# Induced attention and a leaky feed-forward layer: the x blocks of the first pass are loaded from GpSimd's queue instead of SyncE's

## The chip, the cores and the metric

The kernel runs on one core of a Trainium2 chip. The metric is the device time of one execution in microseconds (us). TensorE (PE) multiplies, VectorE (DVE) and ScalarE (ACT) work on tiles, GpSimd (POOL) does a little elementwise work, and SyncE (SP) issues transfers. Each engine takes its own instructions in the order in which they are written; between engines there are semaphores.

## The reference

For each of 4 batches, 32 inducing rows attend over 12,480 tokens and give h; then all tokens attend over the 32 rows of h. The result goes through a feed-forward layer with a leaky ReLU.

```
def mab(q, kv):                       # q: rows x 128, kv: rows x 128
    s = (q @ kv.T) / sqrt(128)
    a = softmax(s)                    # over the rows of kv, 1e-9 added to the sum
    return a @ kv
h = mab(inducing, x)                  # first pass: 32 x 128 per batch
y = mab(x, h)                         # second pass: 12480 x 128 per batch
g = y @ w_in                          # 128 -> 2048
out = maximum(0.01 * g, g) @ w_out    # 2048 -> 128
```

All inputs and outputs are float32: x is 4 x 12480 x 128, `inducing` 32 x 128, `w_in` 128 x 2048, `w_out` 2048 x 128.

## The kernel before

The tokens of a batch are cut into six groups of 2048 and a rest of 192 (RG). A tile of the feed-forward part is 512 tokens, and the hidden width of 2048 is cut into 16 slices. One unit of work u is one slice of one tile: a product into PSUM (`ph`, L705), its positive part on ScalarE (`ghi`, L718), the remainder on VectorE (`glo`, L726), and three products into the output accumulator (`po`, L744). Products run LOOK = 3 units ahead: `ph` has three PSUM buffers, so the product of a unit can't start before VectorE has read the one three units earlier.

The attention of the next batches is woven into these units. For batch 0 an order written out by hand (ORDER) sets every step up to unit 48, and its x comes through `start` (L833). For batches 1 to 3 there are lanes of generators, each stepped once per unit in the main loop (L1217 to L1242): `scores` (the function `first_scores`), `values`, `seconds`, `stacking`, `fetches`, `stores`. A step that yields HEAVY adds to a debt that holds the lanes back for some units. Since the program is written in that order, the place of an instruction in its engine's queue is fixed.

The first pass needs x turned, with its 128 channels on the partitions. `load_blocks` reads x in blocks: for one half of a group (two of its four j) and four bands of 32 channels it issues eight transfers, each of 32 partitions x 16 x 32 elements (64 KB, in runs of 32 elements, 128 B); for RG twelve of 32 x 2 x 32 elements (8 KB). VectorE then turns 32 x 32 squares (`xTr` L389, `xT` L395). The tiles `xc` have three buffers. `first_scores` asks for three halves at once when it begins (RG and the first two: 12 + 16 = 28 transfers) and for one more half after each half that has been turned. That makes 324 transfers in three batches.

The steps of other lanes that the prediction speaks of: in the second pass, GpSimd subtracts the row maximum (`y<-y,mx`, L597), ScalarE takes the exponential (L603), VectorE sums and inverts (`sm`, L607 to L610), GpSimd multiplies (`y<-y,sm`, L612), and VectorE turns the result (`aT`, L621). GpSimd also makes the low parts of the attention weights (`alo`, L644), which SyncE spreads over partitions into `A`. In the first pass GpSimd moves maxima and sums between partition bands in copies of a few elements: `four<-rm` (L303), read by VectorE in L306 or L309; `nm<-nm` (L314), read by ScalarE; `four<-zn` (L497), read by VectorE in L498; `rz<-rz` (L502), read by ScalarE in L509.

SyncE's queue has all transfers but one: rows of x for the value products (L220), the blocks (L248), the spread of `A` (L656) and of `hws` (L560), and the stores of the output (L791). GpSimd issues none.

Of the kernel before, what the change touches and what calls it, by code (L numbers as in the profile page):

```python
# [20 lines left out]
def induced_attention_then_leaky_ffn(  # L21
# [20 lines left out]
    nc = tc.nc  # L42
# [153 lines left out]
    def rows_of(b, g):  # L196
        base, J, K = GROUPS[g]
        return x[b][base : base + 32 * J * K, :]
# [42 lines left out]
    def load_blocks(b, g, j0, nj):  # L241

        _, J, K = GROUPS[g]
        t = sb.tile([P, 32, 32], F32, tag="xc", name="xc", bufs=3)
        src = rows_of(b, g).rearrange("(j r k) c -> r j k c", j=J, k=K)
        for cb in range(NB):
            for j in range(nj):
                nc.sync.dma_start(  # L248
                    t[32 * cb : 32 * cb + 32, j * K : (j + 1) * K, :],
                    src[:, j0 + j, :, 32 * cb : 32 * cb + 32],  # L250
                )
        return t
# [107 lines left out]
    def first_scores(b):  # L360
# [5 lines left out]
        def more():  # L366
            if halves:
                h = halves.pop(0)
                blocks[h] = load_blocks(b, *h)
# [909 lines left out]
```

## Time and profile before

| | |
|---|---|
| median of 3 runs | 1496.11 us (1496.09 to 1496.35) |
| profiled execution | 1496.72 us, span of its instructions 1494.6 us |
| TensorE busy | 1480.1 us, 99% of the span |
| VectorE, ScalarE, GpSimd busy | 85%, 67%, 8% |
| chain that ended last | TensorE 95%, DMA 2%, VectorE 1% |
| block loads (L248) | 324 issues on SyncE, from 100.7 to 874.4 us |

Busy time is the share of the span in which an engine works on an instruction. Waiting, and issuing a transfer, does not count as busy; so GpSimd's 8% is tile work alone.

### The profile page before, as it was taken

The page shows a single profiled execution, that of the slowest core. Times are in us where ns is not written, and L with a number is a line of the kernel's source. Part 1 is how long each engine was busy: PE and PEld are TensorE (multiplying, and loading weights), DVE is VectorE, ACT ScalarE, POOL GpSimd, SP SyncE. Part 2 cuts the span into 40 slices and gives each one's busy share as a digit, 9 for nine tenths or more (in the row PEclk, how much of TensorE's full clock was granted, in tenths as well). Part 3 has the DMA queues.
Part 4 walks back from the last instruction along what each step waited for, and adds up shares of the span by engine and source line. Part 5 has one row for each costly group of instructions (what it writes and reads, how often), then busy time and mean ns, then how long its engine had stood idle before and what let it go on. Part 6 is the DMA issues. An engine that isn't in the chain of part 4 may idle for free.

```text
span 1494.6 us, 22249 instructions
## 1 busy us (share of the span) xinstructions
PE 1480.1 (99%) x7861; PEld 1262.8 (84%) x7861; DVE 1265.5 (85%) x2137; ACT 999.6 (67%) x1748; POOL 112.4 (8%) x182
## 2 busy tenths in 40 slices
PE   8999999999999999999999999999999999999998
PEld 6788888888889888888888888888888898888887
DVE  6888898879898898789899898798888888888886
ACT  5766666666676666676676666676766766666665
POOL 1300100000100100000010100010100000000000
PEclk9999999999999999999999999999999999999999
DMA  8127446335444432243533531231212212212211
GB/s 285 44 56 137 82 78 158 61 59 95 82 103 82 111 82 50 43 96 69 110 69 68 135 67 19 43 73 20 50 34 38 43 25 49 43 24 48 41 26 22
DMA packets 402079, 105.23 MB, mean 70 GB/s; under 512 B 372624, under 2 KB 375088, under 8 KB 401968
## 3 DMA queue, kind: packets, MB, share of 16 engines
q1 hardware_dynamic: 401920, 103.80, 33.7%
q8 instruction: 62, 1.02, 0.3%
q14 instruction: 49, 0.40, 0.1%
q10 hardware_dynamic: 48, 0.02, 0.0%
HBM read 48.94 MB, written 25.56 MB: 50 GB/s over the span
## 4 chain that ended last, share of the span: by engine, by line
PE 95%; DMA 2%; DVE 1%; SPq 1%; ACT 0%; issue 0%; POOL 0%; DVEq 0%; ACTq 0%
PE po L744 67%; PE ph L705 23%; PE s_ps L262 3%; PE po L763 1%; PE h_ps L438 1%; DMA xr<-in_x_dram 1%; DMA raw<-in_moe_w_out_dram 0%; DMA raw<-in_moe_w_in_dram 0%; SPq L248 0%; SPq L833 0%; PE w_ps L1069 0%; DVE glo L726 0%; ACT ghi L718 0%; DMA xc<-in_x_dram 0%; PE hw_ps L545 0%
## 5 line engine op out<-in xcount | busy, mean ns | idle before, releaser
L718 ACT ACTIVATE ghi<-ph 128x512 fp32r<-128x512 f32 (+1 forms) x1568 | 929.5, 595 | 463.7 <-PE ph L705 458.5
L726 DVE SCALAR_TENSOR_TENSOR glo<-ph,ghi 128x512 fp32r<-128x512 f32 (+1 forms) x1568 | 1041.9, 679 | 185.4 <-ACT ghi L718 163.0
L705 PE MATMUL ph<-A,hws 128*128 128x512 f32 (+1 forms) x1600 | 596.6, 377 | 1.6 <-DVE glo L726 1.3
L744 PE MATMUL po<-ghi,w_hi 128*128 128x512 f32 (+1 forms) x1568 | 593.7, 379 | 0.0
L744 PE MATMUL po<-glo,w_hi 128*128 128x512 f32 (+1 forms) x1568 | 593.1, 378 | 0.0
L744 PE MATMUL po<-ghi,w_lo 128*128 128x512 f32 (+1 forms) x1568 | 593.0, 378 | 0.0
L705 PEld LDWEIGHTS ph<-A,hws 128*128 128x128 f32 x1600 | 301.9, 189 | 59.3 <-DVE glo L726 5.6
L744 PEld LDWEIGHTS po<-glo,w_hi 128*128 128x128 f32 x1568 | 296.4, 189 | 41.9 <-DVE glo L726 0.7
L744 PEld LDWEIGHTS po<-ghi,w_lo 128*128 128x128 f32 x1568 | 296.3, 189 | 41.1
L744 PEld LDWEIGHTS po<-ghi,w_hi 128*128 128x128 f32 x1568 | 296.4, 189 | 39.9 <-ACT ghi L718 0.2
L773 DVE STREAM_TRANSPOSE osb<-po 128x512 f32<-128x512 f32 (+1 forms) x98 | 68.8, 702 | 1.5 <-PE po L763 1.5
L644 POOL TENSOR_TENSOR alo<-aT,ahi 128x512 fp32r<-128x512 f32 x22 | 28.1, 1279 | 486.1 <-ACT ahi L639 451.4
L395 DVE STREAM_TRANSPOSE xT<-xc 128x512 f32<-128x512 f32 x72 | 50.5, 701 | 1.6 <-DMA xc<-in_x_dram 1.6
L597 POOL TENSOR_TENSOR y<-y,mx 128x512 f32<-128x512 f32 x23 | 24.2, 1051 | 278.5 <-DVE mx L595 218.7
L612 POOL TENSOR_TENSOR y<-y,sm 128x512 f32<-128x512 f32 x23 | 24.1, 1049 | 189.1 <-DVE sm L610 159.9
L763 PE MATMUL po<-A,m2s 128*128 128x512 f32 (+1 forms) x100 | 37.1, 374 | 0.0
L355 DVE STREAM_TRANSPOSE y<-s_ps 128x512 f32<-128x512 f32 x22 | 15.7, 715 | 10.8 <-PE s_ps L262 9.2
L262 PE MATMUL s_ps<-xT,indT 128*32 128x512 f32 x192 | 24.2, 595 | 0.5 <-ACT xT L871 0.5
L262 PE MATMUL s_ps<-xT,hT 128*32 128x512 f32 x192 | 24.0, 597 | 0.4 <-ACT hT L1013 0.4
L763 PEld LDWEIGHTS po<-A,m2s 128*128 128x128 f32 x100 | 18.9, 189 | 2.6
L280 DVE TENSOR_SCALAR_CACHE_REDUCE e<-s_ps 128x512 f32<-128x512 f32 x18 | 12.4, 690 | 8.3 <-PE s_ps L262 7.5
L438 PE MATMUL h_ps<-xr,ay 128*32 128x128 f32 x576 | 17.6, 274 | 0.0
(152 smaller groups left out, 376.6 us busy)
## 6 DMA issues: line engine op xcount, KB each, us to landing
xr<-in_x_dram SPq DMA_DIRECT2D x96, 256.0 KB, 5.1
out_dram<-osb SPq DMA_DIRECT2D x384, 64.0 KB, 2.2
xc<-in_x_dram SPq DMA_DIRECT2D x288, 64.0 KB, 2.7
A<-ahi SPq DMA_DIRECT2D x188, 64.0 KB, 2.0
A<-alo SPq DMA_DIRECT2D x188, 64.0 KB, 2.0
hws<-hilo SPq DMA_DIRECT2D x64, 64.0 KB, 2.0
raw<-in_moe_w_in_dram SPq DMA_DIRECT2D x4, 512.0 KB, 7.8
raw<-in_moe_w_out_dram SPq DMA_DIRECT2D x4, 512.0 KB, 8.3
```

The lines of the kernel that those rows point to most:

```text
L262: nc.tensor.matmul(dst, lhsT, rhs, start=True, stop=True)
L395: nc.vector.transpose(t[:, j, :], blk.rearrange("p n c -> p (n c)"))
L438: nc.tensor.matmul(hp[32 * k : 32 * k + 32, :C], ay[:rows, 4 * q + k, :], xb[:rows, k, :], start=(i == 0 and q == 0), stop=(last[k] == i a ...
L597: engines[0].tensor_tensor(out=yv, in0=yv, in1=mx[:rows, :K].unsqueeze(2).broadcast_to([rows, K, M]), op=ALU.subtract,)
L612: engines[1].tensor_tensor(out=yv, in0=yv, in1=smv.unsqueeze(2).broadcast_to([rows, K, M]), op=ALU.mult)
L644: (engine or nc.gpsimd).tensor_tensor(out=alo[sl], in0=aT.pop((b, g))[: 32 * J, :], in1=ahi[sl].bitcast(F32), op=ALU.subtract,)
L705: nc.tensor.matmul(ph[:, o : o + w], hw[b][1][:, f * P : (f + 1) * P], woven(A4[t][:, o : o + w], t), start=True, stop=True,)
L718: nc.scalar.activation(halves(ghi[:, :n], t)[1], live[u][2], AF.Relu)
L726: nc.vector.scalar_tensor_tensor(out=halves(glo[:, :n], t)[1], in0=ph, scalar=0.0, in1=halves(ghi[:, :n], t)[1].bitcast(F32), op0=ALU.max, ...
L744: nc.tensor.matmul(accs[t][:, :n], w[:, f, :], woven(r[:, :n], t), start=(f == 0 and w is w_hi and r is live[u][0]), stop=False,)
L763: nc.tensor.matmul(accs[t][:, o : o + w], hw[b][2], woven(a4[:, o : o + w], t), start=False, stop=(o + w == n),)
L773: nc.vector.transpose(osb[:, :n], po[:, :n])
```

## The change

The block loads are issued by GpSimd instead of SyncE. Nothing else is written differently: the same 324 transfers stand at the same places of the program, but now in GpSimd's queue.

```
         for cb in range(NB):
             for j in range(nj):
-                nc.sync.dma_start(
+                nc.gpsimd.dma_start(
                     t[32 * cb : 32 * cb + 32, j * K : (j + 1) * K, :],
                     src[:, j0 + j, :, 32 * cb : 32 * cb + 32],
                 )
```

The instructions of TensorE, VectorE and ScalarE keep their order. On GpSimd, where batch 1's loads begin (`xc` is the block tile, `y` and `yr` the scores of the second pass for a full group and for RG, `mx` and `sm` their maxima and inverse sums):

```order
 L612 TENSOR_TENSOR y<-y,sm 128x512
 L597 TENSOR_TENSOR y<-y,mx 128x512
+L248 DMA xc<-in_x_dram 32x2x32 x12
+L248 DMA xc<-in_x_dram 32x16x32 x16
 L612 TENSOR_TENSOR y<-y,sm 128x512
 L597 TENSOR_TENSOR yr<-yr,mx 96x64
+L248 DMA xc<-in_x_dram 32x16x32 x16
 L612 TENSOR_TENSOR yr<-yr,sm 96x64
+L248 DMA xc<-in_x_dram 32x16x32 x8
 L644 TENSOR_TENSOR alo<-aT,ahi 128x512
+L248 DMA xc<-in_x_dram 32x16x32 x16
 L597 TENSOR_TENSOR y<-y,mx 128x512
```

The multiplication L612 of a tile now stands behind the 28 loads with which batch 1 begins. On GpSimd, where batch 2's loads begin (`nm` and `zn` are batch 1's negated maximum and its sum, `rz` the inverse of the sum):

```order
 L303 TENSOR_SCALAR four<-rm 32x2 x4
 L314 COPY nm<-nm 32x1 x3
+L248 DMA xc<-in_x_dram 32x2x32 x12
+L248 DMA xc<-in_x_dram 32x16x32 x16
 L497 COPY four<-zn 32x1 x4
 L502 COPY rz<-rz 32x1 x3
```

The 28 loads stand between the copies of the maximum and the copies of the sum; it is the same where batch 3's begin. On SyncE, at the place of batch 1's first loads (`out_dram` is the output, `osb` its tile, `xr` the rows for the value products):

```order
 L791 DMA out_dram<-osb 256x2x32 x8
-L248 DMA xc<-in_x_dram 32x2x32 x12
-L248 DMA xc<-in_x_dram 32x16x32 x16
 L220 DMA xr<-in_x_dram 96x256
 L220 DMA xr<-in_x_dram 128x512 x6
 L791 DMA out_dram<-osb 256x2x32 x4
 L220 DMA xr<-in_x_dram 128x512 x2
```

The rows and stores behind the loads move up by 28 places.

## Rows read from the trace of the kernel before

**Rows 1.** The page, part 1: busy us (share of the span) and instructions of each engine.
```profile
PE 1480.1 (99%) x7861; PEld 1262.8 (84%) x7861; DVE 1265.5 (85%) x2137; ACT 999.6 (67%) x1748; POOL 112.4 (8%) x182
```

**Rows 2.** Busy time by stretch: start:end, length, then engines, clock, DMA share, GB/s.
```profile
core 0: us, PE busy (x) PEld busy (x) DVE busy (x) ACT busy (x) POOL busy (x), PEclk, DMA share, GB/s
...
95.00:320.00 225.00, 223.94 (x1243) 190.16 (x1243) 197.41 (x347) 149.28 (x264) 18.18 (x41) 1.00 0.49 95
320.00:620.00 300.00, 300.00 (x1642) 256.36 (x1642) 261.61 (x451) 200.49 (x356) 25.46 (x49) 1.00 0.42 83
620.00:960.00 340.00, 339.93 (x1811) 288.86 (x1813) 294.20 (x497) 227.85 (x398) 26.17 (x48) 1.00 0.37 75
```

**Rows 3.** Waits, all engines: who waited for whom, us in total, times, longest.
```profile
DVE xT L395 <- DMA xc<-in_x_dram: 1.6, 1, 1.6
...
ACT ahi L639 <- DMA A<-ahi: 1.4, 1, 1.4
```

**Rows 4.** Line L248: ns min/median/max of an issue on SyncE, first and last start.
```profile
L248 SPq DMA_DIRECT2D xc<-in_x_dram x324: 571/625/3000, 100.7 to 874.4; - x162
```

**Rows 5.** DMA issues: KB each, median us from issue to landing.
```profile
xc<-in_x_dram SPq DMA_DIRECT2D x288, 64.0 KB, 2.7
```

**Rows 6.** Timeline of GpSimd: start us, us, line, [idle before <-releaser].
```profile
99.34 1.05 POOL L597 TENSOR_TENSOR y<-y,mx 128x512 f32<-128x512 f32 x1 [35.58 <-PE po L744]
105.31 1.05 POOL L612 TENSOR_TENSOR y<-y,sm 128x512 f32<-128x512 f32 x1 [4.92 <-DVE sm L610]
...
131.07 0.29 POOL L612 TENSOR_TENSOR yr<-yr,sm 96x64 f32<-96x64 f32 x1 [15.68 <-DVE sm L610]
140.49 1.28 POOL L644 TENSOR_TENSOR alo<-aT,ahi 128x512 fp32r<-128x512 f32 x1 [9.13 <-ACT ahi L639]
160.28 1.05 POOL L597 TENSOR_TENSOR y<-y,mx 128x512 f32<-128x512 f32 x1 [18.51 <-DVE mx L595]
161.41 1.06 POOL L303 TENSOR_SCALAR four<-rm 32x3 f32<-32x3 f32 x4
...
200.48 1.28 POOL L644 TENSOR_TENSOR alo<-aT,ahi 128x512 fp32r<-128x512 f32 x1 [13.59 <-ACT ahi L639]
...
240.85 0.61 POOL L314 COPY nm<-nm 32x1 f32<-32x1 f32 x3 [4.48 <-DVE least L309]
...
297.44 0.61 POOL L314 COPY nm<-nm 32x1 f32<-32x1 f32 x3 [6.34 <-DVE least L309]
304.78 0.82 POOL L497 COPY four<-zn 32x1 f32<-32x1 f32 x4 [6.72 <-DVE zn L335]
...
592.11 0.61 POOL L314 COPY nm<-nm 32x1 f32<-32x1 f32 x3 [4.39 <-DVE least L309]
```

**Rows 7.** Timeline of all engines around the first place.
```profile
107.77 0.38 PE L705 MATMUL ph<-A,hws 128*128 128x512 f32 x1
...
108.56 0.70 DVE L621 STREAM_TRANSPOSE aT<-y 128x512 f32<-128x512 f32 x1
...
109.19 2.05 DVE L726 SCALAR_TENSOR_TENSOR glo<-ph,ghi 128x512 fp32r<-128x512 f32 x3
...
110.58 0.38 PE L705 MATMUL ph<-A,hws 128*128 128x512 f32 x1
```

**Rows 8.** Timeline of VectorE: the other instructions that read GpSimd's results, and L389.
```profile
117.41 0.37 DVE L389 STREAM_TRANSPOSE xTr<-xc 128x192 f32<-128x192 f32 x1
...
166.43 0.14 DVE L306 TENSOR_REDUCE nm<-four 32x1 f32<-32x12 f32 x1
...
316.93 0.13 DVE L498 TENSOR_REDUCE rz<-four 32x1 f32<-32x4 f32 x1
...
617.00 0.13 DVE L498 TENSOR_REDUCE rz<-four 32x1 f32<-32x4 f32 x1
```

**Rows 9.** Timeline of SyncE: the first block loads, and a spread of A.
```profile
100.73 19.27 SPq L248 DMA_DIRECT2D xc<-in_x_dram  x28
...
149.55 0.58 SPq L656 DMA_DIRECT2D A<-ahi  x1
```

More of the change, by code (lines that the diff above doesn't have):

```diff
@@ L247, in load_blocks @@
             for j in range(nj):
-                nc.sync.dma_start(
+                nc.gpsimd.dma_start(
                     t[32 * cb : 32 * cb + 32, j * K : (j + 1) * K, :],
```

## The prediction

> **What bounds the kernel now.** I read the page's busy times first, then the busy time by stretch, then the waits, and then the timelines of GpSimd and VectorE, because the change concerns a queue and a queue is read by who stands behind whom. TensorE is busy for 1480.1 of 1494.6 us and GpSimd for 112.4 [rows 1]. In the stretch in which the block loads run, from 95 to 960 us, TensorE has 1.06, 0.00 and 0.07 us that are not busy [rows 2]. So that stretch can hardly get shorter than it is; it can only get longer, if something makes TensorE wait. The loads keep nobody waiting: one transpose of VectorE waited once for a block, 1.6 us [rows 3].
>
> What makes TensorE wait is VectorE or ScalarE standing still, since both work in order. How long it can do without VectorE is read at 108.56 us [rows 7]: VectorE turns a tile there (0.70 us) and reaches its next `glo` at 109.19. That one frees the `ph` buffer filled at 107.77, which TensorE fills again at 110.58. The `glo` is done at about 109.19 + 0.68 = 109.87 (a third of the 2.05 for three). So 0.7 us of a halt are free and the rest stops TensorE. Time lost so isn't won back, as TensorE has no slack to catch up with.
>
> **The change, part by part.** *Removed:* 324 issues from SyncE, at a median of 625 ns [rows 4], about 200 us of its queue. Rows of x, stores and the spread of `A` behind them go out earlier. Who waits for these: ScalarE, 1.4 us in all, for a spread [rows 3]. TensorE's idle time in the stretch is 1.13 us [rows 2], so this is worth between 0 and 1.1 us; I take 0.
>
> *Added:* 324 issues on GpSimd. Its 8% says nothing of their cost; what counts is how long each holds the queue, p, and who stands behind. No row shows p. From below, the smallest GpSimd instructions follow each other at 1.06 / 4 = 0.27 us (L303) [rows 6], and SyncE takes 0.63 for this very load [rows 4]. From above: a load of 64 KB is 512 runs of 128 B, each to be described once to read and once to write; if GpSimd does that as two of its dearest passes over 512 elements, L644 at 1.28 [rows 6], p is 2.56. I take 1.05, the row of GpSimd's commonest pass over 512 elements (L597, L612), which lies nearest to the middle of 0.63 and 1.28, and the same for small loads, as a low bound and a high bound at SyncE differ little (571 and 625 ns).
>
> The Trainium skill ("DMA: Bandwidth & Descriptors", section Specifications) says that a transfer from GpSimd, whose descriptors are written by software, has its first byte after about 1 us, against about 0.6 from SyncE. The second agrees with the 0.63 us of rows 4; no run here shows the first. By it p would be 1.0 as an estimate, and the sum below 33.3 us instead of 37.4.
>
> Each load also waits for the load eight before it to land, as GpSimd's transfers share eight semaphores. Landing takes 2.7 us from SyncE [rows 5]; eight loads at 1.05 take 8.4, which covers it. If landing takes over 8.4 us, p rises to an eighth of it.
>
> *First place, batch 1 begins.* L597 ends at 99.34 + 1.05 = 100.39 [rows 6]. Then come 28 loads, then L612 (1.05), whose result VectorE needs at 108.56 for L621 [rows 7]. Before, L612 started at 105.31 and was in time. Now it ends at 101.44 + 28p, and with 0.7 us free, TensorE loses 28p - 7.8. At p = 1.05 that is 21.6 us.
>
> *Second place, batch 2 begins.* The copies of `nm` end at 297.44 + 0.61 = 298.05 [rows 6]. 28 loads, then L497 (0.82), which VectorE's L498 needs at 316.93 [rows 8]. Before, L497 stood there at 304.78, 11 us early. The loss is 298.05 + 28p + 0.82 - 316.93 - 0.7 = 28p - 18.8, that is 10.6 us.
>
> *Third place, batch 3 begins.* The same with 592.11 + 0.61 = 592.72 and 617.00 [rows 6, 8]: 28p - 24.2, that is 5.2 us. The stalls before shift all engines alike, so the differences hold.
>
> *Fourth place, batch 1's first maximum.* After the first stall everything is later by 28p - 7.8. The next loads wait for a block buffer that L389 frees, at 117.41 + 0.37 + 28p - 7.8 = 110.0 + 28p [rows 8]. Behind that GpSimd has 16 loads, L612 (0.29), 8 loads, L644 (1.28), 16 loads, L597 (1.05) and four copies L303 (1.06) [rows 6]: it ends at 113.7 + 68p. VectorE reads them in L306 at 166.43 + 28p - 7.8, with 0.7 free: 159.3 + 28p. The loss is 40p - 45.6, at p = 1.05 less than nothing, so 0; the cover is thin (3.6 us) and gone at p = 1.14. The spread of `A` behind L644 is in time: L644 ends at 111.5 + 52p = 166.1, SyncE comes to it at 149.55 + 21.6 = 171.2 [rows 9].
>
> *The other groups* have 8 to 24 loads between instructions of GpSimd that lie some 15 to 40 us apart; at 1.05 us a load I take 0. The tightest that I worked out, before batch 1's second maximum: L644 ends at 200.48 + 1.28 = 201.76, then come 24 loads, L597 (1.05) and four copies L303 (about 1.06 again), which VectorE's L309 reads just before 240.85 [rows 6]. With 0.7 free that binds from p = (240.85 + 0.7 - 203.9) / 24 = 1.57.
>
> Sum: 21.6 + 10.6 + 5.2 + 0 = 37.4 us on the profiled execution's own 1496.72, so 1534.1. That execution lies 0.6 above the median of the runs, which gives 1533.5.
>
> **The rivals.**
>
> *No change (the other side).* If an issue on GpSimd is as cheap as its smallest instruction, the first place loses 28 x 0.27 - 7.8 < 0 and so do the others: 1496, not slower. It decides at p = 7.8 / 28 = 0.28 us. For it: GpSimd is busy for 112 us of 1494.6 [rows 1], and a queue that only hands work on could be this quick. Against it: SyncE, with nothing else to do, takes 0.63 for the same load [rows 4]. A gain of over 0.2% (3.0 us, about what a measurement of this kernel can tell from no change) has no place to come from, as the idle time in the stretch is 1.1 us [rows 2].
>
> The Trainium skill (the same page, section Issuing engines are not separate DMA queues) says that spreading transfers over issuing engines saves only issue time, which is usually small. The 200 us taken off SyncE are that time, and rows 3 show nobody waiting for it. By that rule alone the result would be this rival.
>
> *GpSimd issues as fast as SyncE.* With p = 0.63 only the first place binds: 28 x 0.63 - 7.8 = 9.8 us, 1506. For it: the engine only tells the transfer engines what to do, and SyncE's time hardly depends on the size (571 to 625 ns). Against it: GpSimd's other instructions are slower than their counterparts, 1.05 us for a pass over 512 elements against VectorE's 0.70 [rows 6, 7].
>
> *The price grows with the runs.* 512 runs to read and 512 to write make p well above 1.28. Then the fourth place and the groups with 24 loads bind as well. At 1.28 the sum is 28.0 + 17.0 + 11.6 + 5.6 = 62 us; at 1.7 it is 39.8 + 28.8 + 23.4 + 22.4 + 24 x (1.7 - 1.57) = 117 us, 1614; at 2.56 it is 63.9 + 52.9 + 47.5 + 56.8 + 23.8 = 245 us, 1741. For it: these are the shortest runs in the kernel, and the count of 512 is far above a row load's. Against it: at SyncE the count of runs shows nothing.
>
> The Trainium skill ("SBUF — State Buffer", section SBUF: two separate sides) says that GpSimd can't write descriptors while VectorE runs an instruction in a two-port mode, which would lengthen p by up to one such instruction. The rows at 108 us show VectorE's passes over 512 elements at 0.68 to 0.70 us, none of them in half the time, so I give the rule no weight of its own.
>
> **How the numbers follow.** Between p = 0.8 and 1.35 (first place binding strongly, others partly) lies my forecast, with 0.55. GpSimd about as fast as SyncE, 0.4 to 0.8: 0.15. The price growing with the runs, above 1.35: 0.21. No change, below 0.38 (loss under 3 us): 0.06. A gain: 0.03, for something that I don't see. The likeliest case's own range is 0.8 to 1.35: the first place loses 14.6 to 30.0 us, the second 3.6 to 19.0, the third 0 to 13.6, the fourth 0 to 8.4, so 18 to 71 us, 1514 to 1567. The range that holds 8 in 10 goes from p = 0.57, SyncE's lowest row (28 x 0.57 - 7.8 = 8.2 us, 1504), to p = 1.7 (1614); beyond lie the cases without change and the tail up to 1741. Slower by over 0.2%: 0.55 + 0.15 + 0.21 = 0.91; within 0.2%: 0.06; faster: 0.03.
>
> **What the profile after would show.** Right: L248 stands on GpSimd's queue, its issues 0.8 to 1.35 us apart; VectorE's L621 at about 108 us waits some 20 us for L612, and L498 waits in batches 1 and 2; in the same stretches TensorE shows gaps of that size, and before 95 us and after 960 nothing changes. TensorE's clock may fall in a gap of 20 us; the granted clock before was 1.00 in all three stretches [rows 2], and a lower one behind the gap would add to my sum, which has no term for it. Wrong would be: issues of 0.3 us or less and no wait at L621; waits of VectorE's L395 for blocks, which would say that landing and not issuing is the cost; or stalls at L306 and L309 as large as at L621, which would say that p is above 1.5.

## The result, and the profile after

| | before | after |
|---|---|---|
| median | 1496.1 us (1495.65 to 1496.35, 4 runs) | 1508.0 us (1506.43 to 1509.51, 4 runs) |
| ratio after to before | | 1.0084, 95% interval 1.0072 to 1.0096 |
| span of the profiled execution | 1494.6 us | 1506.8 us |

The change costs 11.9 us. The direction was as predicted and the time lies in the range; the size was a third of the 37.4 us forecast.

The busy times first, on the page of the changed kernel; they answer to [rows 1].

```profile
PE 1482.7 (98%) x7861; PEld 1264.5 (84%) x7861; DVE 1266.4 (84%) x2137; ACT 1000.0 (66%) x1748; POOL 316.9 (21%) x506
```

GpSimd has 324 instructions and 204.5 us more: on this engine an issue counts as busy. TensorE has 2.6 us more for the same 7861 products, part of it at a lower clock, as will be seen. The same three stretches as in [rows 2]:

```profile
95.00:320.00 225.00, 214.66 (x1133) 181.66 (x1131) 188.94 (x330) 142.24 (x252) 95.99 (x161) 0.97 0.41 91
320.00:620.00 300.00, 300.00 (x1663) 256.27 (x1665) 261.69 (x451) 200.26 (x356) 98.79 (x167) 1.00 0.39 84
620.00:960.00 340.00, 339.93 (x1846) 289.44 (x1834) 293.06 (x495) 227.34 (x397) 78.94 (x133) 1.00 0.34 75
```

TensorE stands still for 10.34 us in the first stretch, against 1.06 before, and its clock there is 0.97. The other two are as they were. Of these stretches only the first lost time. Who waited there (waits of VectorE and TensorE, with the total, the count and the longest):

```profile
DVE aT L621 <- POOL y L612: 11.1, 1, 11.1
...
PE ph L705 <- DVE glo L726: 11.4, 2, 10.3
```

This is the predicted first place and its chain: VectorE's transpose waits for GpSimd's multiplication, and TensorE for the `glo` behind the transpose. There is no wait of VectorE's L498, L306 or L309 among the waits, and none of its L395 for a block. What an issue costs on GpSimd (compare [rows 4]; ns as minimum, median and maximum); the last two lines say what it stood idle for in front of issues:

```profile
L248 POOL DMA_DIRECT2D xc<-in_x_dram x324: 533/651/745, 99.5 to 885.8; - x162
...
  DVE xT L395: 94.7, 19
...
  DMA xc<-in_x_dram: 1.2, 1
```

A median of 651 ns, where SyncE took 625, and never over 745. The 94.7 us are waits for a free block buffer; no wait of another engine goes back to them. GpSimd's timeline (compare [rows 6]):

```profile
98.53 1.05 POOL L597 TENSOR_TENSOR y<-y,mx 128x512 f32<-128x512 f32 x1 [35.58 <-PE po L744]
99.52 6.10 POOL L248 DMA_DIRECT2D xc<-in_x_dram  x11
105.80 3.11 POOL L248 DMA_DIRECT2D xc<-in_x_dram  x5 [0.18 <-issue]
110.13 7.69 POOL L248 DMA_DIRECT2D xc<-in_x_dram  x12 [1.21 <-DMA xc<-in_x_dram]
117.84 1.06 POOL L612 TENSOR_TENSOR y<-y,sm 128x512 f32<-128x512 f32 x1
...
162.47 5.14 POOL L248 DMA_DIRECT2D xc<-in_x_dram  x8 [2.63 <-DVE xT L395]
...
309.23 16.64 POOL L248 DMA_DIRECT2D xc<-in_x_dram  x28
325.92 0.83 POOL L497 COPY four<-zn 32x1 f32<-32x1 f32 x4
...
603.89 16.65 POOL L248 DMA_DIRECT2D xc<-in_x_dram  x28
620.59 0.83 POOL L497 COPY four<-zn 32x1 f32<-32x1 f32 x4
```

The 28 loads of the second and third place take 16.64 us, 0.594 each: the 16 large ones (64 KB, 512 runs) at 5.14 / 8 = 0.643, and so the twelve small ones (64 runs) at (16.64 - 10.28) / 12 = 0.53. At the first place the same 28 hold the queue from 99.52 to 117.84, 18.3 us or 0.654 each, with a wait of 1.21 us for an earlier load to land. VectorE's side of the three places (compare [rows 7, 8]):

```profile
118.93 0.71 DVE L621 STREAM_TRANSPOSE aT<-y 128x512 f32<-128x512 f32 x1 [11.10 <-POOL y L612]
...
328.17 0.13 DVE L498 TENSOR_REDUCE rz<-four 32x1 f32<-32x4 f32 x1
...
628.22 0.13 DVE L498 TENSOR_REDUCE rz<-four 32x1 f32<-32x4 f32 x1
```

At the second place L497 ends at 326.75, 1.4 us before VectorE comes to L498; at the third at 621.42, 6.8 us before. TensorE at the first place:

```profile
109.55 0.38 PE L763 MATMUL po<-A,m2s 128*128 128x512 f32 x1
120.27 0.80 PE L705 MATMUL ph<-A,hws 128*128 128x512 f32 x1 [10.34 <-DVE glo L726]
120.86 0.63 PE L744 MATMUL po<-ghi,w_hi 128*128 128x512 f32 x1
```

Its products take 0.63 us behind the gap instead of 0.38. The clock by short stretches (columns as in [rows 2]; the clock is the third number from the end):

```profile
110.00:113.00 3.00, 0.00 (x0) 0.00 (x0) 0.00 (x0) 0.00 (x0) 2.87 (x5) 0.87 0.26 56
113.00:116.00 3.00, 0.00 (x0) 0.00 (x0) 0.00 (x0) 0.00 (x0) 3.00 (x6) 0.50 0.44 104
...
122.00:124.00 2.00, 2.00 (x6) 1.55 (x6) 1.61 (x3) 0.60 (x1) 0.00 (x0) 0.50 0.00 0
124.00:126.00 2.00, 2.00 (x7) 1.59 (x6) 0.83 (x2) 0.60 (x1) 0.00 (x0) 0.53 0.55 86
126.00:130.00 4.00, 4.00 (x20) 3.52 (x19) 2.84 (x6) 2.79 (x5) 0.29 (x1) 1.00 0.65 154
```

The clock fell to its lower level (0.50, 1.2 GHz) while TensorE stood still, and TensorE ran at it until about 126.

How the span's 12.2 us come together, by the times at which the same instruction starts in both traces. L597 is 0.8 us early (98.53 against 99.34 in [rows 6]), which is start-up. The product behind the gap is 9.7 us late (120.27 against 110.58 in [rows 7]): the gap cost 10.5. VectorE's L389, which comes when the clock is back, is 12.6 us late (117.41 in [rows 8]):

```profile
129.97 0.37 DVE L389 STREAM_TRANSPOSE xTr<-xc 128x192 f32<-128x192 f32 x1
```

So the low clock cost 12.6 - 9.7 = 2.9. Then 1.3 us are won back: GpSimd's L314 is 11.2 us late at 308.67 (297.44 in [rows 6]). Of these, 1.06 are a halt that the kernel before has in its trace and the changed one has not. There VectorE waited for a block and TensorE for the `glo` behind it:

```profile
137.44 0.71 DVE L395 STREAM_TRANSPOSE xT<-xc 128x512 f32<-128x512 f32 x1 [1.60 <-DMA xc<-in_x_dram]
...
138.78 0.48 PE L705 MATMUL ph<-A,hws 128*128 128x512 f32 x1 [1.06 <-DVE glo L726]
```

L314 is still 11.2 us late at 603.34 (592.11), and so is VectorE's L498 at the second and third place (328.17 against 316.93, 628.22 against 617.00 in [rows 8]): these two places add nothing. The last 1.0 us comes late in the program, where no block load is left.

### The profile page after: what moved, and what is told of

It is laid out like the page before. It is cut to its first block, busy times and chain, and to the rows that moved or that the text cites. A ratio compares the mean times of both kernels' runs of the same rounds, so it can differ in the third digit from the quotient of the medians.

```text
span 1506.8 us, 22337 instructions
## 1 busy us (share of the span) xinstructions
PE 1482.7 (98%) x7861; PEld 1264.5 (84%) x7861; DVE 1266.4 (84%) x2137; ACT 1000.0 (66%) x1748; POOL 316.9 (21%) x506
## 2 busy tenths in 40 slices
DMA packets 257504, 105.24 MB, mean 70 GB/s; under 512 B 222864, under 2 KB 225904, under 8 KB 257392
## 3 DMA queue, kind: packets, MB, share of 16 engines
q0 software_dynamic: 10368, 19.19, 6.1%
## 4 chain that ended last, share of the span: by engine, by line
PE 95%; DMA 2%; POOL 1%; DVE 1%; ACT 1%; SPq 0%; issue 0%; DVEq 0%; ACTq 0%
PE po L744 66%; PE ph L705 23%; PE s_ps L262 2%; PE po L763 1%; PE h_ps L438 1%; POOL xc L248 1%; DMA raw<-in_moe_w_out_dram 0%; DMA xr<-in_x_dram 0%; DMA raw<-in_moe_w_in_dram 0%; DMA xc<-in_x_dram 0%; SPq L833 0%; PE w_ps L1069 0%; PE h_ps L966 0%; DVE glo L726 0%; PE hw_ps L545 0%
## 5 line engine op out<-in xcount | busy, mean ns | idle before, releaser
L705 PE MATMUL ph<-A,hws 128*128 128x512 f32 (+1 forms) x1600 | 597.5, 377 | 11.7 <-DVE glo L726 11.4
L248 POOL DMA_DIRECT2D xc<-in_x_dram x324 | 204.8, 640 | 102.9 <-DVE xT L395 94.7
L597 POOL TENSOR_TENSOR y<-y,mx 128x512 f32<-128x512 f32 x23 | 24.2, 1052 | 229.0 <-DVE mx L595 169.2
L395 DVE STREAM_TRANSPOSE xT<-xc 128x512 f32<-128x512 f32 x72 | 50.5, 701 | 0.0
L612 POOL TENSOR_TENSOR y<-y,sm 128x512 f32<-128x512 f32 x23 | 24.2, 1051 | 123.5 <-DVE sm L610 101.1
L303 POOL TENSOR_SCALAR four<-rm 32x2 f32<-32x2 f32 (+1 forms) x36 | 7.6, 211 | 92.0 <-DVE e L280 90.0
L621 DVE STREAM_TRANSPOSE aT<-y 128x512 f32<-128x512 f32 x24 | 16.9, 702 | 11.1 <-POOL y L612 11.1
L262 PE MATMUL s_ps<-xT,indT 128*32 128x512 f32 x192 | 24.2, 595 | 0.5 <-ACT xT L871 0.5
```

Of the source, the lines that this page charges most:

```text
L248: nc.gpsimd.dma_start(t[32 * cb : 32 * cb + 32, j * K : (j + 1) * K, :], src[:, j0 + j, :, 32 * cb : 32 * cb + 32],)
L262: nc.tensor.matmul(dst, lhsT, rhs, start=True, stop=True)
L395: nc.vector.transpose(t[:, j, :], blk.rearrange("p n c -> p (n c)"))
L597: engines[0].tensor_tensor(out=yv, in0=yv, in1=mx[:rows, :K].unsqueeze(2).broadcast_to([rows, K, M]), op=ALU.subtract,)
L612: engines[1].tensor_tensor(out=yv, in0=yv, in1=smv.unsqueeze(2).broadcast_to([rows, K, M]), op=ALU.mult)
L705: nc.tensor.matmul(ph[:, o : o + w], hw[b][1][:, f * P : (f + 1) * P], woven(A4[t][:, o : o + w], t), start=True, stop=True,)
```

## The experiments

Theory A: the loss is one instruction, L612, that stands behind 28 issues on GpSimd; an issue costs about 0.6 us; the other places have room. Theory B: the loads on GpSimd cost by themselves, wherever they stand. All were timed beside runs of the kernel before (medians 1496.32 in the first four, 1496.58 in the last four).

**Only the 28 loads of the first place back on SyncE.** The other 296 stay on GpSimd. Against the changed kernel:

```
-    def load_blocks(b, g, j0, nj):
+    def load_blocks(b, g, j0, nj, eng=None):
-                nc.gpsimd.dma_start(
+                (eng or nc.gpsimd).dma_start(
-                blocks[h] = load_blocks(b, *h)
+                first = b == 1 and len(blocks) < 3
+                blocks[h] = load_blocks(b, *h, eng=nc.sync if first else nc.gpsimd)
```

> Only the 28 loads with which batch 1 begins go back to SyncE; the other 296 stay on GpSimd. Theory A (order in GpSimd's queue at one place: L612 stands behind 28 loads, about 0.62 us each): the wait of VectorE at L621 is gone, no other place binds, 1496 to 1497.5 us. Theory B (every load costs a little, by slower landing, by transfers of two queues side by side, or by GpSimd disturbing VectorE): 296 of 324 shares of 11.9 us stay, about 1507 us.

Measured: 1494.78 us, ratio 0.9991 (0.9983 to 1.0000), 1.2 us below the range expected. Busy time by stretch, the first:

```profile
95.00:320.00 225.00, 225.00 (x1266) 189.72 (x1265) 197.49 (x346) 148.38 (x263) 86.42 (x149) 1.00 0.45 94
```

No gap, clock 1.00, no wait at the transpose. 28 of the 324 loads carry the whole loss.

**Only these 28 on GpSimd.** The reverse edit, with the same parameter `eng`:

```
-                blocks[h] = load_blocks(b, *h)
+                first = b == 1 and len(blocks) < 3
+                blocks[h] = load_blocks(b, *h, eng=nc.gpsimd if first else nc.sync)
```

> The reverse: only the 28 loads with which batch 1 begins are on GpSimd, 296 on SyncE. Theory A: the whole loss stays, 1507 to 1509 us, with VectorE waiting about 11 us at L621. Theory B: 28 of 324 shares, about 1497 us.

Measured: 1508.25 us, ratio 1.0079 (1.0067 to 1.0092). The waits (the edit adds one line, so L621 is L622 here):

```profile
DVE aT L622 <- POOL y L613: 12.3, 1, 12.3
...
PE ph L706 <- DVE glo L727: 12.6, 2, 11.6
```

The whole loss is here. VectorE waits 12.3 us, where the changed kernel has 11.1; one load waited 2.2 us here for an earlier one to land.

**Every load cut in two.** 648 issues of half the size, so a block costs about twice the queue time. The prediction's sum is tried at the price that it assumed. Against the changed kernel:

```
-                nc.gpsimd.dma_start(
-                    t[32 * cb : 32 * cb + 32, j * K : (j + 1) * K, :],
-                    src[:, j0 + j, :, 32 * cb : 32 * cb + 32],
-                )
+                for k in (0, K // 2):
+                    nc.gpsimd.dma_start(
+                        t[32 * cb : 32 * cb + 32, j * K + k : j * K + k + K // 2, :],
+                        src[:, j0 + j, k : k + K // 2, 32 * cb : 32 * cb + 32],
+                    )
```

> Each load is cut into two of half the runs, so that the queue is held about twice as long for the same bytes (648 issues of 32 or 256 runs; estimate from the changed kernel's rows, 0.53 us a small and 0.645 a large load: 0.52 and 0.59 for the halves). That is about the price per block of the prediction. Theory A with the prediction's places: 28 loads are 24 x 0.52 + 32 x 0.59 = 31.4 us; first place 31.4 - 7.8 = 23.6, second 12.6, third 7.2, fourth 80 x 0.59 - 45.6 = 1.6, plus about 1.5 us of lower clock behind each of the long gaps: 45 to 50 us, 1541 to 1546 us. If only the first place can bind: 1521 us. Theory B (a cost per issue, 11.9 us for 324): 1520 us, and no long waits at L498.

Measured: 1546.89 us, 50.6 more than before, ratio 1.0344 (1.0329 to 1.0360), 0.9 us above the range expected. The waits (lines one on from the prediction's):

```profile
DVE aT L622 <- POOL y L613: 24.7, 1, 24.7
DVE rz L499 <- POOL four L498: 19.1, 2, 12.4
...
DVE nm L307 <- POOL four L304: 2.7, 1, 2.7
...
PE ph L706 <- DVE glo L727: 44.0, 5, 24.0
```

And GpSimd at the third place:

```profile
632.63 30.27 POOL L249 DMA_DIRECT2D xc<-in_x_dram  x56
```

That is 1.08 us for a block, in two issues of 0.54. At p = 1.08, 30.3 us for 28 blocks, the prediction's formulas give 30.3 - 18.8 = 11.5 and 30.3 - 24.2 = 6.1 for the second and third place. With the 0.7 us that are free VectorE should wait 12.2 and 6.8; it waits 12.4 and 19.1 - 12.4 = 6.7. The first place, where the loads end 32.0 us after L597 (98.76 to 130.71 on GpSimd), gives 32.0 - 7.8 = 24.2, and TensorE's longest wait is 24.0. So three steps of the sum hold to 0.3 us at this price. The fourth place binds too: large blocks cost 2 x 0.576 = 1.15 there (32 issues in 18.43 us), just over the 1.14 worked out, and VectorE's L306 (L307 here) waits 2.7 us, 2.0 beyond the free 0.7, where 40p - 45.6 gives 0.4; where the other 1.6 come from wasn't tried. TensorE's waits make 44.0 of the 50.6 us; the clock behind the gaps, 0.94 on average in the first stretch, is in the rest.

**The twelve small loads of the first place on SyncE**, the 16 large ones on GpSimd. It asks for the point from which the place binds. Against the changed kernel, with the parameter `eng`:

```
-                blocks[h] = load_blocks(b, *h)
+                rest = b == 1 and len(blocks) < 1
+                blocks[h] = load_blocks(b, *h, eng=nc.sync if rest else nc.gpsimd)
```

> Of the 28 loads with which batch 1 begins, the 12 small ones go to SyncE and the 16 large ones stay on GpSimd, as all others. Theory A: 16 x 0.645 = 10.3 us in the queue, 10.3 - 7.8 = 2.5 us of TensorE's time; the granted clock does not fall in so short a gap, so 1498 to 1499.5 us. If the clock costs its 1.5 us behind any gap: 1500 us. Theory B: about 1507.5 us.

Measured: 1499.05 us, ratio 1.0016 (1.0007 to 1.0025). GpSimd's timeline:

```profile
99.20 10.49 POOL L248 DMA_DIRECT2D xc<-in_x_dram  x16
109.71 1.06 POOL L613 TENSOR_TENSOR y<-y,sm 128x512 f32<-128x512 f32 x1
```

The 16 hold the queue for 10.49 us, 0.656 each, with no wait for a landing among them. VectorE's and TensorE's waits:

```profile
DVE aT L622 <- POOL y L613: 3.3, 1, 3.3
...
PE ph L706 <- DVE glo L727: 3.7, 2, 2.5
```

And the clock by short stretches:

```profile
110.00:112.00 2.00, 0.00 (x0) 0.00 (x0) 1.19 (x2) 0.00 (x0) 0.77 (x1) 1.00 1.04 165
112.00:114.00 2.00, 1.85 (x7) 1.57 (x8) 1.99 (x5) 0.96 (x2) 0.00 (x0) 0.81 0.96 244
114.00:118.00 4.00, 4.00 (x14) 3.30 (x13) 2.31 (x4) 1.62 (x4) 0.00 (x0) 0.67 1.01 270
118.00:122.00 4.00, 4.00 (x20) 3.49 (x20) 3.43 (x8) 2.80 (x5) 0.85 (x2) 1.00 0.71 149
```

VectorE waits 3.3 us and TensorE 2.5: the 0.7 us that are free are here too (3.3 - 0.7 = 2.6). The place follows the count of issues in front of L612. One part of the expectation did not hold: the clock fell also behind this short gap, after the work had begun again. This is one execution. Of the eleven, the five with a mean granted clock of 0.999 took 1497.32 to 1498.51 us, and the six with 0.997 or 0.998, the profiled one among them, 1499.05 to 1499.99; so it isn't shown that the clock fell in each.

**All 324 loads on GpSimd, the waiting multiplication on VectorE.** `second` is the generator of a tile's second pass; its last argument names the engines for L597 and L612. Against the changed kernel:

```
-        ] + [second(0, g) for g in [2, RG, 3, 4, 5]]
+        ] + [second(0, 2, [nc.gpsimd, nc.vector])] + [second(0, g) for g in [RG, 3, 4, 5]]
```

> All 324 loads stay on GpSimd's queue, the 28 of batch 1's beginning at the same place; only the multiplication L612 of the one tile that stood behind them is done by VectorE. Theory A (the time goes into one instruction standing behind the 28 loads in GpSimd's order): L621 no longer waits, TensorE shows no gap at about 110 us, VectorE has one more pass of about 0.7 us; 1495 to 1497.5 us. Theory B (the loads on GpSimd cost by themselves, through contention, through later landing or through GpSimd's other work): the gap or its equal stays, 1505 to 1509 us.

Measured: 1495.09 us, ratio 0.9993 (0.9984 to 1.0002). VectorE's timeline:

```profile
106.33 0.68 DVE L612 TENSOR_TENSOR y<-y,sm 128x512 f32<-128x512 f32 x1
...
108.13 0.70 DVE L621 STREAM_TRANSPOSE aT<-y 128x512 f32<-128x512 f32 x1
```

L621 has no wait in front of it. Busy time by stretch, the first:

```profile
95.00:320.00 225.00, 225.00 (x1262) 190.81 (x1264) 198.83 (x349) 149.87 (x265) 101.86 (x176) 1.00 0.44 95
```

The 28 loads stand where they stood, from 99.83 to 118.76 us, and cost nothing. So it is not the loads but what is behind them; theory B falls.

**The same edit without the change** (all loads on SyncE, the multiplication on VectorE):

> The kernel before (all loads on SyncE) with the same one multiplication L612 on VectorE: what that edit does by itself. Both theories: within 1 us of the kernel before, 1495 to 1497.5 us.

Measured: 1495.66 us, ratio 0.9996 (0.9987 to 1.0005). The edit by itself does nothing that can be measured, so what lies between the changed kernel and the experiment above is the wait and the clock behind it.

**Only batch 3's loads on GpSimd.** Against the kernel before:

```
-                nc.sync.dma_start(
+                (nc.gpsimd if b == 3 else nc.sync).dma_start(
```

> Only batch 3's 108 loads on GpSimd, the other 216 on SyncE. The third place keeps some 7 us to spare at 0.59 us a load. Theory A: no wait at L498, 1495 to 1497.5 us, as before. Theory B (each load costs something on GpSimd, a third of the whole loss for a third of the loads): 1499 to 1501 us.

Measured: 1495.42 us, ratio 0.9997 (0.9988 to 1.0006). GpSimd at the third place:

```profile
591.29 16.77 POOL L248 DMA_DIRECT2D xc<-in_x_dram  x28
608.10 0.82 POOL L497 COPY four<-zn 32x1 f32<-32x1 f32 x4
```

A third of the loads, none of the loss: the third place has room.

**The changed kernel again**, beside the last three:

> The changed kernel as it is, beside the three others: 1506 to 1510 us by both theories; L621 waits 10 to 12 us for L612, and TensorE's clock falls behind the gap as it did.

Measured: 1507.93 us, ratio 1.0081 (1.0067 to 1.0095). TensorE's timeline behind the gap:

```profile
120.19 0.80 PE L705 MATMUL ph<-A,hws 128*128 128x512 f32 x1 [10.29 <-DVE glo L726]
```

VectorE's, when the clock is back:

```profile
129.75 0.37 DVE L389 STREAM_TRANSPOSE xTr<-xc 128x192 f32<-128x192 f32 x1
```

The same gap, and the low clock costs 129.75 - 117.41 = 12.3 less 120.19 - 110.58 = 9.6, that is 2.7. At 308.46 GpSimd's L314 is 11.0 us late (297.44 before), so 1.3 are won back here too. Only 0.4 us of the span's 11.4 come later, so the 1.0 us of the first trace isn't shown to be the change's.

No version is shown to be faster than the kernel before: the three that are free of the wait and have loads on GpSimd have ratios of 0.9991 to 0.9997, with intervals that reach 1.0.

## Why the prediction was right in its direction and wrong in its size

- *What bounds the kernel; that there is nothing to gain.* Right as far as the times can tell. SyncE lost 324 issues, and with the wait gone the ratios are 0.9991 and 0.9993, with intervals that reach 1.0. One reading was wrong: that the loads keep nobody waiting. The 1.06 us in which TensorE is not busy are the halt at 138.78, behind VectorE's wait of 1.6 us for a block. The changed kernel's traces haven't got it, but neither has that of the multiplication on VectorE with all loads on SyncE (TensorE busy for 225.00 of 225.00 us), so it isn't shown that the change took it away.
- *The price p of an issue on GpSimd.* This is the step that failed. I took 1.05 us, from the time of a pass over 512 elements, as it lay near the middle between SyncE's issue of this load (0.63) and GpSimd's dearest pass (1.28). Measured is 0.594 over the 28 loads, 0.53 for a small and 0.643 for a large one: SyncE's price (0.571 to 0.625) within some 7 per cent. [rows 9] even had these 28 loads on SyncE, 19.27 us; put in for 28p they give 11.5 us at the first place. A row of the same operation on another engine was nearer than a row of another operation on the same engine. That 28 issues stand in each term made an error of 0.46 us one of 12.8 us at each place.
- *First place.* Right as a mechanism, too large as a number. 28p - 7.8 with the 18.3 us that the queue was held is 10.5; the gap cost 10.5. It was 21.6 in the sum.
- *Second and third place.* Right as formulas and on the wrong side of their thresholds. At 0.594 they give 16.6 - 18.8 = -2.2 and 16.6 - 24.2 = -7.6; the trace shows 1.4 and 6.8 us to spare, and with the 0.7 us free 2.1 and 7.5. The halved loads made both bind, by what the formulas say. So 15.8 us of the sum went here.
- *Fourth place and the other groups.* Nothing, as predicted. With the halved loads the fourth cost 2.0 us at 1.15, where the formula has 0.4, so it binds somewhat earlier than at the 1.14 worked out.
- *The landing cover.* Right at the assumed price, not at the true one. Eight loads take 4.4 us here instead of 8.4, and one took longer to land. The chain of waits of the changed kernel at the first place:

```profile
99.58 4.37 POOL xc L248 x8
103.95 5.90 DMA xc<-in_x_dram
```

  The load issued at about 104, one of the twelve small ones, had landed only 5.9 us later, against a median of 2.2 for these on the page of the changed kernel, and the load eight places behind it waited 1.21 us for it. That, a pause of 0.18 us and issues that took 0.3 us more in sum, is the 18.3 - 16.6 = 1.7 us that the first place loses beyond p. The transfer engines were busy by 0.83 from 107 to 110 us. SyncE's seven loads of rows, which went out at 120.04 before, behind the 28 loads, now go out beside them:

```profile
99.92 4.54 SPq L220 DMA_DIRECT2D xr<-in_x_dram  x7
```

  Whether it was these that held the load up wasn't tried.
- *The clock.* The prediction named it and had no term for it. It cost 2.9 us, and 2.7 in the repeat; the halt of 1.06 us in the trace before, which neither of these two has, hides a part of it in the spans.
- *Start-up and end.* 0.8 us early and 1.0 late in this trace, 0.9 and 0.4 in the repeat; they aren't shown to be the change's.
- *The rivals.* What happened is the rival "GpSimd issues as fast as SyncE", priced at 9.8 us and given 0.15. At the measured price its formula gives 8.8; with what the first place lost beyond p (1.7) and the clock (2.9, less the 1.3 won back behind it) that is 12.1, and measured are 11.9. The likeliest case's own range, 1514 to 1567, does not hold the time; the wide one does, since it began at SyncE's lowest row. No change by p below 0.28 fell at the first row of issues. The price growing with the runs fell as well: eight times the runs make 0.53 into 0.643. On the Trainium skill's two rules ("DMA: Bandwidth & Descriptors"): the price of 1.0 us that I had worked out from its first byte (section Specifications) isn't what the queue shows, 0.594. Nor could the 0.63 us of [rows 4] agree with the Trainium skill's 0.6: the row has how long an issue holds SyncE's queue, and no row has the time to a first byte. Large loads land in a median of 2.6 us from GpSimd against 2.7 from SyncE. The rule that the issuing engine saves only issue time (section Issuing engines are not separate DMA queues) holds for the gain, of which the times show none, and says nothing of the compute behind the issues on an engine that has some.

## What to carry to other kernels

Issuing a transfer from an engine that also computes puts the issue time in front of everything behind it in that engine's order. The busy share of that engine, 8% here, said nothing of it; find the bursts of issues, the next compute instruction behind each, and how early its result was ready before, and compare that lead with the count of issues times their price. For a price that the trace doesn't show, take the nearest row of the same operation before one of another kind, and where the sum has thresholds, work out on which side of each the two ends of the price fall.

## What the runs showed of the hardware that was not expected

- An issue on GpSimd costs nearly what one on SyncE does, and depends little on the runs: 0.53 us for 64 runs of 128 B, 0.54 a piece for the mixture of halved loads, 0.643 for 512 runs; SyncE's minimum and median are 0.571 and 0.625 [rows 4].
- The clock fell behind a gap of 2.5 us, in the one trace of it, as behind one of 10.3 us. Behind the long one TensorE began at the lower level and stayed there until about 126 us, nearly 6 us in. Behind the short one it began at the full clock, and its products took 0.63 us each from 113.39 to 116.38 us and 0.38 again from 116.75; the granted clock was 0.81 from 112 to 114 us, 0.67 from 114 to 118 us and 1.00 after.
- The packets of all queues fell from 402,079 to 257,504 at the same bytes (105.23 and 105.24 MB); the queue that only the changed kernel has shows 10,368 packets for 19.19 MB.
